# A fused attention and gated MLP kernel: a token moved to TensorE's queue, maxima turned by VectorE, a projection in 64-row tiles

## The chip, the cores and the metric

The kernel runs on one core of a Trainium2 chip. The core has five engines that work beside each other, each with its own instruction queue: TensorE (matmuls; PE in the profile, its weight loads PEld), VectorE (DVE), ScalarE (ACT), GpSimd (POOL) and SyncE (SP, which here only issues DMAs). They wait for each other through semaphores. Matmul results land in PSUM, which has eight banks of 128 x 512 numbers of 32 bits.

The metric is device time of one execution in microseconds. Three runs of the kernel before took 1590.16, 1590.88 and 1591.05; their median is 1590.88.

## The reference

Two branches read the same normalised rows. One is attention with 32 heads of 16 columns over 2048 rows, then a projection; the other is an MLP whose output gates the first.

```python
xn = _layernorm(x)                                  # x: 1 x 2048 x 512
q, k, v = split(xn @ wqkv)                          # 32 heads of 16
p = softmax(einsum("bhqd,bhkd->bhqk", q, k) * 16 ** -0.5)
s = einsum("bhqk,bhkd->bhqd", p, v) @ wo            # 512 x 512
g = silu(gelu(xn @ w1 + b1) @ w2 + b2)              # 512 x 1376 x 512
return x + s * g
```

## The kernel before, in words

Products of numbers of 32 bits are made from high and low parts: three matmuls (high by high, high by low, low by high) in the fast 32-bit form, summed in one PSUM bank. For scores the three products stand above each other in the contraction, 3 x 16 = 48 rows, so that one score matmul has 48 rows and uses one *row tile*, the upper or the lower 64 rows of TensorE's array (`a` = 0 or 1). [...]

The attention is cut into 32 *units* `u`: a group of four heads (`GH`), eight groups (`NG`), and a chunk of 512 query rows, four chunks (`NCH`). For a unit every score is made twice:

- **S**: queries on PSUM's partitions, keys along the columns, 128 x 512. VectorE takes the maximum of each half row (L185, `s_max`), and the maxima of a unit are reduced and negated (`nm`, L240) and split into high and low parts by POOL (`nmh`, L243 and L244).
- **T**: keys on the partitions, queries along the columns, with two more rows in the contraction (50 rows) that subtract the maximum of each query. ScalarE takes the exponential (L724, `t_one`). The result `PT` is multiplied with the values (**V**, L787, `pv_step`), four matmuls with 128 rows and 17 columns, side by side in columns; the seventeenth column gives the denominator.

For T the maxima must lie along a row, so the 128 x 32 tile `nmh` of a unit is turned. `s_end1` (L259) does this with a TensorE matmul against the identity into a PSUM bank, and `s_end2` copies the bank to SBUF (L265 by ScalarE during the first stage, L267 by VectorE later) and stores it to a scratch tensor `mh_d` (L268). `load_mh` later reads the two rows into the query tile `QT`. When `s_end1` runs is counted: a finished unit is put in `later` with a number of ticks.

There are three stages:

1. **First stage** (to about 480 us): layer norm, the matmuls for q, k, v and the MLP, in 64-row tiles, two row tiles interleaved by hand (`run`, `mm`, L573). `fill` puts S matmuls (`LEAD` = 144 steps' worth) between them when a count of matmuls is due; `ROWS` is the total of that count, and a turn in `fill` takes two places of it (`put`).
2. **Attention stage**: a loop over `n` of 512 steps. Each step works off a string of letters, `ORDER`: `TSXTTSTYV` while S remain to be made, `TTTTV` after. Four T make up one key block of a unit, V is the product for the step before. Of the three S tiles that a step makes, two are whole (S: both matmuls of a pair come at different places, one on each row tile) and the third is cut in halves: X writes one half of a bank from row tile 0, Y the other half from row tile 1. [...] This order is a *token*: an empty instruction on POOL (L217) that waits for X, and Y waits for it. POOL's small work on the maxima (`put_off`) is queued behind the token.
3. **Projection**: from step `DONE` = 492 the S are done. The first `NW` = 10 blocks of 128 rows are multiplied with `wo` inside the loop, each in two steps, with full 128-row matmuls (`w_mul`, L79), six a step after its four T. `load_gx` fetches the gate and the rows of x into a ring of four `gx` tiles, `w_token` rounds the attention output into high (ScalarE, L854) and low parts (POOL, L855), `gate` makes the silu factor (L847, L848), `w_out` multiplies from PSUM (VectorE, L883), adds x (POOL, L888) and stores. The other six blocks are done in the last steps and behind the loop.

Between V and the projection the denominators are handled: `o_move` moves them, `o_den` inverts them and sends each of four heads' rows back to 16 partitions with a DMA of its own (L819), `o_div` multiplies (L824).

The order on each engine is the order in which the program issues. PSUM banks are taken in turn: three for S (`s_tile`, `s_ring`), four for T (`t_tile`), one for V. A turn in the attention stage takes one of the T banks, one in the first stage one of the S banks.

Of the kernel before, what the change touches and what calls it, by code (L numbers as in the profile page):

```python
# [8 lines left out]
F32 = mybir.dt.float32  # L9
F32R = mybir.dt.float32r  # L10
AF = mybir.ActivationFunctionType
# [5 lines left out]
P = 128  # L17
S = 2048
D = 512
H = 32  # L20
DH = 16
KT = D // P
NT = S // P
CH = 512
NCH = S // CH
F = 1376
FT = (F + P - 1) // P
GH = 4
# [4 lines left out]
LEAD = 144  # L33
NW = 10
EARLY = 4
DONE = 492
FILL0 = 38
# [4 lines left out]
KB = 3  # L42
# [5 lines left out]
def fused(ctx: ExitStack, tc: tile.TileContext, x, wqk, wv, wo, w1, b1, w2, b2, out):  # L48
    nc = tc.nc
# [14 lines left out]
    den_d = dpool.tile([NG * NCH, GH, CH], F32, name="den_d")  # L64
    mh_d = dpool.tile([NG * NCH, 2, GH, CH], F32, name="mh_d")

    ident_r = keep.tile([P, P], F32R, name="ident_r")
# [13 lines left out]
            if then:  # L81
                then()

    QS, QT, MX, NM, MH = {}, {}, {}, {}, {}
    SYNC = mybir.DependencyInfo(mybir.DependencyClass.Sync, mybir.DependencyReason.DATA)
    qss = []
    NU = NG * NCH
# [3 lines left out]
    def s_tile(held=False):  # L91
        pool = s_ring.pop(0)
        if not held:
            s_ring.append(pool)
        return pool.tile([P, CH], F32, name="ps"), pool
# [57 lines left out]
    made = [0, 0]  # L153
    done = {u: 0 for u in range(NU)}
    later, ended, errands, sent = [], [], [], set()
# [5 lines left out]
    def flush():  # L161
        while later and later[0][0] <= 0:
            u = later.pop(0)[1]
            run_off()
            s_end1(u)
            s_end2(u)

    def at_of(job):
        u, st, p = job
# [24 lines left out]
    def s_whole(job, a):  # L194
        ps = s_tile()[0]
        s_mm(ps, job, a, 0, 0, CH)
        s_max(ps, job, a, slice(0, 2))
# [5 lines left out]
    jobs, whole, cut, put_off = [], [], [], []  # L203

    def s_op(op):
        if op == "S":
            if whole:
                s_whole(whole.pop(), 1)
            else:
                whole.append(jobs.pop(0))  # L210
                s_whole(whole[0], 0)
        elif op == "X":
            if not cut:
                cut[:] = [jobs.pop(0), 0]
            ps, pool = s_tile(True)
            x = s_mm(ps, cut[0], 0, 0, cut[1] * HC, HC)
            token = nc.gpsimd.nop().ins  # L217
            tc.add_manual_dep(token, x.name, SYNC, reason="row tile done")
            cut[2:] = [ps, pool, token]
            run_off()  # L220
        else:
            job, n, ps, pool, token = cut
            y = s_mm(ps, job, 1, HC, n * HC, HC)
            tc.add_manual_dep(y, token.name, SYNC, reason="other row tile")
            s_max(ps, job, slice(0, 2), n)
            s_ring.append(pool)
            cut[1] += 1
            if n:
                cut.clear()

    def run_off():
        while put_off:
            put_off.pop(0)()
# [21 lines left out]
    prog = {}  # L255

    def s_end1(u):
        pm = s_tile()[0] if "seen" in prog else t_tile()
        nc.tensor.matmul(pm[:2 * GH * NCH, :P], NM.pop(u).rearrange("p i a -> p (i a)"), ident_r, start=True, stop=True)  # L259
        MH[u] = pm  # L260

    def s_end2(u):
        mh = qring.tile([2 * GH * NCH, P], F32, name="mh", bufs=1)
        if "seen" in prog:
            nc.scalar.activation(mh, MH.pop(u)[:2 * GH * NCH, :P], AF.Copy)  # L265
        else:
            nc.vector.tensor_copy(mh, MH.pop(u)[:2 * GH * NCH, :P])  # L267
        nc.sync.dma_start(mh_d[u].rearrange("i j (q s) -> (i j q) s", s=P), mh)  # L268
        sent.add(u)

    sa = ExitStack()
# [19 lines left out]
    VQ = 3  # L291
    first = [[("v", t // NCH, t % NCH) for t in range(i, i + 4)] for i in range(NT - 4 * VQ, NT, 4)]
    qs = [(2, 0), (2, 2)] + [(g, 0) for g in range(3, NG)] + [(g, 2) for g in range(3, NG)]
    nu, pairs = len(ms) // 2, []
# [8 lines left out]
    for j in range(len(pairs)):  # L303
        for h in range(2):
# [4 lines left out]
            due = next((i for i in range(j, len(pairs)) if is_m[i]), len(pairs))  # L309
# [4 lines left out]
            n = 2 if nd < len(parts) and parts[nd][2] and ready - nd > room else 1  # L314
            n = max(n, need - 2 * (left - 1))
            while nd < ready and n > 0:
                c, f, k = parts[nd]
# [204 lines left out]
    qring = ctx.enter_context(tc.tile_pool(name="qring", bufs=2, side="right"))  # L522
# [16 lines left out]

    prog.update(n=0, pe=0, seen=0)  # L540
    writer = {}
    s_when, put, row = [], [0], [0, 0]
    ndown = sum(1 for e in plan if e[0] == "down")
    ROWS = 12 * (4 * VQ + 2 * len(pairs)) + 6 * ndown - 10 + 2 * LEAD - 2 * (LEAD // 16 - 1) - FILL0

    def fill(a):
        due = FILL0 + put[0] + sum(made) * ROWS // (4 * LEAD)
        if sum(made) < 4 * LEAD and row[a] >= due and (made[0] <= made[1]) == (a == 0):
            taken()
            if later and later[0][0] <= 0:  # L550
                put[0] += 2
                u = later.pop(0)[1]
                s_end1(u)
                s_end2(u)
                return
            s_one(a)
            row[a] += 1
            tick()

    def taken():  # L560
        prog["pe"] += 1
        s_when.append(prog["pe"])
        if len(s_when) > 2:
            prog["seen"] = max(prog["seen"], s_when[-3])
# [142 lines left out]
    def t_tile():  # L707
        turns[0] += 1
        if turns[0] < 5:
            pool = (ps_m, ps_x, ps_a, ps_b)[turns[0] - 1]  # L710
        else:
            pool = ps_m if turns[0] % 4 == 1 else ps_t
        return pool.tile([P, CH], F32, name="pst" if pool is ps_t else "ps")
# [46 lines left out]
    wb = ctx.enter_context(tc.tile_pool(name="work_b", bufs=2))  # L760
# [4 lines left out]
    wo_h = kp.tile([P, KT, D], F32R, name="wo_h")  # L765
    wo_l = kp.tile([P, KT, D], F32R, name="wo_l")

    WR = {}

    def load_wo(k):  # L770
        WR[k] = wb.tile([P, 2, D], F32, name="gx", bufs=4)[:, 0]
        nc.sync.dma_start(WR[k], wo[k * P:(k + 1) * P, :])

    def wo_high(k):
# [5 lines left out]
    PV, OS, DN, DR = {}, {}, {}, {}  # L780
# [18 lines left out]
    def o_rows(u, j):  # L799
        g, c = divmod(u, NCH)  # L800
        r0 = 64 * (g % 2) + DH * j
        return slice(r0, r0 + DH), c, g // 2
# [10 lines left out]
    def o_den(u):  # L813
        dr = DR.pop(u)
        nc.vector.reciprocal(dr, dr)
        nc.sync.dma_start(den_d[u].rearrange("j (a i) -> (j a) i", i=GH * CH // P), dr)
        DN[u] = wb.tile([P, CH], F32, name="dn", bufs=1)
        for j in range(GH):
            nc.sync.dma_start(DN[u][o_rows(u, j)[0]], den_d[u, j:j + 1].to_broadcast([DH, CH]))  # L819

    def o_div(u, eng):
        g, c = divmod(u, NCH)
# [3 lines left out]
    GX, OTS, PW, homes = {}, {}, {}, {}  # L826

    def home(i):
        if i not in homes:
            homes[i] = (slot(i, (P, KT, D)) if i < KB else  # L830
                        keep_r.tile([P, 2 * KT, D], F32, name="kt0"))
        return homes[i]

    def load_gx(t):
        i = 2 * (t % NCH)
        if t < NW:
            GX[t] = wb.tile([P, 2, D], F32, name="gx", bufs=4)
        elif t < NT - NCH:
            GX[t] = home(KB)[:, i:i + 2]
        else:  # L840
            GX[t] = home(1 + i // KT)[:, i % KT:i % KT + 2]
        nc.sync.dma_start(GX[t][:, 0], g_d[t * P:(t + 1) * P, :])
        nc.sync.dma_start(GX[t][:, 1], x[t * P:(t + 1) * P, :])
# [4 lines left out]
        nc.vector.scalar_tensor_tensor(g, e, 1.0, g, op0=OP.add, op1=OP.mult)  # L848

    def w_round(blocks, src, lo):  # L850
        oh = wb.tile([P, KT, P], F32R, name="oh", bufs=3)
        ol = wb.tile([P, KT, P], F32R, name="ol", bufs=3)
        n = len(blocks)
        nc.scalar.activation(oh[:, :n], src, AF.Copy)  # L854
        lo.tensor_sub(ol[:, :n], src, oh[:, :n].bitcast(F32))  # L855
        for i, b in enumerate(blocks):
            OTS[b] = (oh[:, i], ol[:, i])
# [12 lines left out]
    def w_mul(t, ks, parts=(0, 1)):  # L870
        if t not in PW:
            PW[t] = [ps_t.tile([P, CH], F32, name="pst") if NW <= t < NT - NCH or i else
                     ps_m.tile([P, CH], F32, name="ps") if t == NT - 1 else s_tile()[0]
                     for i, cs in enumerate(cols(t))]
        for i, cs in enumerate(cols(t)):
            if i in parts:
                for k in ks:
                    mm3(PW[t][i][:, :cs.stop - cs.start], OTS[t, k], (wo_h[:, k, cs], wo_l[:, k, cs]),
                        k == 0, k == KT - 1)

    def w_gate(t, i=0):
        gx, cs = GX[t], cols(t)[i]
# [14 lines left out]
    def at(n, f, *a, pos=3):  # L897
        todo.setdefault((n, pos), []).append((f, a))

    KS = tuple(range(KT))  # L900
# [21 lines left out]
            at(16 * u + (31 if u < NU - 2 else 22), o_div, u, nc.gpsimd)  # L922
    T3 = range(NT - NCH, NT)
    late = range(NW, NT)
    for t in range(NW):
        n = DONE + 2 * t
        at(n - 4, load_gx, t)
        at(n - 2, w_token, t)
        at(n, w_mul, t, KS[:2])
        at(n, gate, t)  # L930
        at(n + 1, w_mul, t, KS[2:])
        at(n + 1, w_out, t, nc.gpsimd)
    for i, t in enumerate(late):
        n = L - 2 * len(late) - 1 + 2 * i
        at(n - 4, load_gx, t)
# [8 lines left out]
    for n in range(L + 1):  # L944
        ua, ka = divmod(n, 16)
        want = due(n) - due(n - 1)
        i = 0
# [71 lines left out]
```

## Time and profile before

| what | us |
|---|---|
| median of three runs | 1590.88 |
| the profiled execution, whole | 1589.65 |
| its span, first to last instruction | 1587.9 |
| first exponential of the attention stage (L724) | 480.2 |
| last one | 1562.8 |
| turns of maxima (L259), 32, each on TensorE | 0.247 |
| POOL tokens (L217), 490, each | 0.017 |

The span lies 1.75 us inside the profiled execution's time. In a row of the timeline the columns are the start in us, the duration in us (of all merged instructions, if there are several), the engine (with q for its sequencer), the line, the operation, the tiles written and read, the shapes, a count, and in brackets the idle time of the engine before it and what ended that. A matmul's form `48*128 48x256` means 48 rows, 128 weight columns and 256 streamed columns. The end of a matmul is modelled, and matmuls overlap, so starts are safer than durations. In a row of the windows view, busy microseconds of each engine are followed by the count of instructions, and at the end stand the granted clock, the DMA share and GB/s. In a row for one source line, three durations (least, median, most, in ns) are followed by the first and last start.

### The profile page before, as it was taken

Reading aid. Unit: us, or ns where it says so; the run is one execution under the profiler, and the core shown is the slowest. Engines: PE = TensorE matmul, PEld = TensorE weight load, DVE = VectorE, ACT = ScalarE, POOL = GpSimd, SP = SyncE. Lnnn points to the kernel's source line nnn. Section 1 sums busy time; section 2 is a strip of 40 time slices with the busy share of each in tenths; the row PEclk is TensorE's granted clock in tenths of the full one; section 3 lists DMA queues with packets and bytes.
Section 4 is the critical chain, followed back from the end, with each engine's and each line's share of the span. In section 5 each row is a group of like instructions: output and inputs, shape, how many; then the busy total and the mean of one; then the engine's idle time right before and its main releaser. Section 6 shows DMA issues by size and latency. Waiting matters only on the chain.

```text
span 1587.9 us, 32482 instructions
## 1 busy us (share of the span) xinstructions
PE 1577.7 (99%) x12146; PEld 954.9 (60%) x12146; DVE 1382.6 (87%) x2267; ACT 1256.4 (79%) x2524; POOL 378.7 (24%) x398
## 2 busy tenths in 40 slices
PE   9999999999999999999999999999999999999998
PEld 7899989999995444444444444444444444444445
DVE  7489888888988999999999999999999999999734
ACT  4333433444339999999999999999999999999984
POOL 4145575755641001001100200100010000000144
PEclk9999999999999999999999999999999999999999
DMA  6625443354422113111511411221141111110262
GB/s 206 150 59 138 131 137 98 127 154 127 130 83 75 39 33 70 31 36 35 86 31 31 69 35 37 53 49 29 27 78 26 31 29 37 35 29 22 65 198 89
DMA packets 76798, 116.93 MB, mean 74 GB/s; under 512 B 25156, under 2 KB 26436, under 8 KB 75464
## 3 DMA queue, kind: packets, MB, share of 16 engines
q1 hardware_dynamic: 73180, 102.42, 23.4%
q0 software_dynamic: 3264, 12.35, 4.1%
q8 instruction: 96, 1.57, 0.4%
q14 instruction: 62, 0.51, 0.1%
q10 hardware_dynamic: 196, 0.07, 0.0%
HBM read 84.35 MB, written 25.97 MB: 69 GB/s over the span
## 4 chain that ended last, share of the span: by engine, by line
PE 98%; DVE 1%; DMA 0%; issue 0%; ACT 0%; SPq 0%; DVEq 0%; POOLq 0%; ACTq 0%
PE pv L787 32%; PE pst L722 22%; PE ps L573 13%; PE ps L179 9%; PE pst L573 7%; PE ps L722 7%; PE ps L79 4%; PE pv L573 2%; PE pst L79 1%; DVE slot L74 0%; DMA xt<-in_x 0%; DVE st L407 0%; PE pst L259 0%; PE ps L259 0%; DVE xn L421 0%
## 5 line engine op out<-in xcount | busy, mean ns | idle before, releaser
L185 DVE TENSOR_REDUCE mx<-ps 128x2 f32<-128x512 f32 x2048 | 1299.3, 685 | 137.3 <-PE ps L179 53.3
L724 ACT ACTIVATE slot<-pst 128x512 f32<-128x512 f32 x1533 | 833.3, 612 | 5.6 <-PE ps L179 1.1
L787 PE MATMUL pv<-slot,vsb 128*17 128x512 f32 (+1 forms) x4096 | 539.2, 598 | 0.0
L179 PE MATMUL ps<-kt,slot 48*128 48x512 f32 x1364 | 383.6, 370 | 0.1
L722 PE MATMUL pst<-qt,kt 50*128 50x512 f32 x1149 | 380.1, 431 | 0.5 <-DVE gt L655 0.3
L722 PEld LDWEIGHTS pst<-qt,kt 50*128 50x128 f32 x1149 | 191.5, 184 | 264.7 <-ACT slot L724 250.6
L724 ACT ACTIVATE slot<-ps 128x512 f32<-128x512 f32 x515 | 314.8, 612 | 10.3 <-PE pst L722 7.4
L179 PEld LDWEIGHTS ps<-kt,slot 48*128 48x128 f32 x1364 | 225.1, 184 | 2.1 <-POOLq L217 0.4
L573 PE MATMUL ps<-slot,w1h 64*128 64x512 f32 x1088 | 220.4, 393 | 0.0
L179 PE MATMUL ps<-kt,qz 48*128 48x512 f32 x512 | 214.7, 420 | 0.0
L179 PE MATMUL ps<-slot,slot 48*128 48x512 f32 x598 | 167.8, 368 | 0.0
L722 PE MATMUL ps<-qt,kt 50*128 50x512 f32 x387 | 164.1, 426 | 0.0
L573 PEld LDWEIGHTS ps<-slot,w1h 64*128 64x128 f32 x1088 | 153.0, 185 | 6.8 <-ACT junk L587 1.0
L573 PE MATMUL ps<-slot,w1l 64*128 64x512 f32 x544 | 143.0, 393 | 0.0
L367 POOL TENSOR_TENSOR hl<-hg,hh 128x512 fp32r<-128x512 f32 x76 | 96.9, 1298 | 131.5 <-ACT hh L366 92.6
L722 PE MATMUL pst<-qt,slot 50*128 50x512 f32 x384 | 120.1, 426 | 0.0
L787 PEld LDWEIGHTS pv<-slot,vsb 128*17 128x17 f32 (+1 forms) x4096 | 68.7, 96 | 82.8 <-issue 29.4
L587 ACT ACTIVATE junk<-ident_r 1x1 f32<-1x1 f32 x92 | 18.0, 196 | 126.1 <-PE pst L573 122.9
L722 PEld LDWEIGHTS ps<-qt,kt 50*128 50x128 f32 x387 | 71.1, 184 | 75.5 <-ACT slot L724 57.7
L722 PEld LDWEIGHTS pst<-qt,slot 50*128 50x128 f32 x384 | 65.9, 184 | 78.0 <-ACT slot L724 73.0
L179 PEld LDWEIGHTS ps<-kt,qz 48*128 48x128 f32 x512 | 93.7, 183 | 17.9 <-DVE mx L185 0.6
L179 PEld LDWEIGHTS ps<-slot,slot 48*128 48x128 f32 x598 | 98.7, 184 | 1.0
(150 smaller groups left out, 1659.4 us busy)
## 6 DMA issues: line engine op xcount, KB each, us to landing
raw<-in_w SPq DMA_DIRECT2D x88, 256.0 KB
qk_h<-hh SPq DMA_DIRECT2D x32, 256.0 KB
qk_l<-hl SPq DMA_DIRECT2D x32, 256.0 KB
qt<-qk_h SPq DMA_DIRECT2D x128, 64.0 KB
slot<-qk_h SPq DMA_DIRECT2D x92, 64.0 KB
xt<-in_x SPq DMA_DIRECT2D x16, 256.0 KB
g_d<-gt POOLq DMA_DIRECT2D x16, 256.0 KB, 3.0
qt<-qk_l SPq DMA_DIRECT2D x64, 64.0 KB
```

The costliest lines, as they stand in the source:

```text
L79: nc.tensor.matmul(ps, lhs[a], rhs[b], start=first and n == 0, stop=last and n == 2)
L179: return nc.tensor.matmul(ps[:, c0:c0 + w], QS[u][r, p, qi * P:(qi + 1) * P], kts[u // NCH % KB][p][r, k0:k0 + w], start=True, stop=True).ins
L185: nc.vector.tensor_reduce(MX[u][:, 2 * p:2 * p + 2, qi, ki][:, heads, parts], ps.rearrange("p (n c) -> p n c", c=HC), axis=AX.X, op=OP.max)
L367: nc.gpsimd.tensor_sub(hl, raw, hh.bitcast(F32))
L573: i = nc.tensor.matmul(ps, lhs[r], rhs[r], start=first, stop=last).ins
L587: i = nc.scalar.activation(junk[:, :1], ident_r[:1, :1].bitcast(F32), AF.Copy).ins
L722: nc.tensor.matmul(ps, kts[g % KB][p][r, k * P:(k + 1) * P], QT[u][r, p, :], start=True, stop=True)
L724: nc.scalar.activation(PT[u, k][:, 2 * p + a, :], ps, AF.Exp, scale=SCALE)
L787: nc.tensor.matmul(PV[u][32 * j:32 * j + w, :], vsb[:, k, h:h + w], PT[u, k][:, j, :], start=(k == 0), stop=(k == NT - 1))
```

## The change

Four things change.

- **The token.** X no longer issues an empty instruction on POOL. Y issues one on TensorE, directly ahead of its own matmul; it waits for X, and Y waits for it.
- **The turn.** `s_end1` turns the tile with one VectorE transpose of 128 x 32, which turns each block of 32 x 32 by itself, straight into SBUF; the store to `mh_d` follows that layout with pieces of 32 numbers. The matmul, the PSUM bank, the copy and `s_end2` go, and in `fill` the turn takes no places of the count any more.
- **The projection.** Blocks go in pairs over four steps. `w_half` issues the contraction in 64-row halves, row tile 0 for one block of the pair and row tile 1 for the other, four halves behind each of the step's first three T; after two steps the row tiles swap, behind a token on POOL (`turned`). The two blocks use two S banks.
- **Buffers and DMAs.** The ring of `gx` has three tiles and that of `oh` and `ol` four; every fourth block's `gx` goes elsewhere. The four broadcast DMAs of a unit's denominators become one.

```diff
@@ s_op
             x = s_mm(ps, cut[0], 0, 0, cut[1] * HC, HC)
-            token = nc.gpsimd.nop().ins
-            tc.add_manual_dep(token, x.name, SYNC, reason="row tile done")
-            cut[2:] = [ps, pool, token]
+            cut[2:] = [ps, pool, x]
             run_off()
         else:
-            job, n, ps, pool, token = cut
+            job, n, ps, pool, x = cut
+            token = nc.tensor.nop().ins
+            tc.add_manual_dep(token, x.name, SYNC, reason="row tile done")
             y = s_mm(ps, job, 1, HC, n * HC, HC)
             tc.add_manual_dep(y, token.name, SYNC, reason="other row tile")
@@ s_end1, s_end2
     def s_end1(u):
-        pm = s_tile()[0] if "seen" in prog else t_tile()
-        nc.tensor.matmul(pm[:2 * GH * NCH, :P], NM.pop(u).rearrange("p i a -> p (i a)"), ident_r, start=True, stop=True)
-        MH[u] = pm
...
+        mh = qring.tile([P, 2 * GH * NCH], F32, name="mh", bufs=1)
+        nc.vector.transpose(mh, NM.pop(u).rearrange("p i a -> p (i a)").bitcast(F32))
+        nc.sync.dma_start(mh_d[u].rearrange("i j (q b s) -> b (i j q) s", b=NCH, s=2 * GH * NCH), mh)
         sent.add(u)
@@ fill
-    ROWS = 12 * (4 * VQ + 2 * len(pairs)) + 6 * ndown - 10 + 2 * LEAD - 2 * (LEAD // 16 - 1) - FILL0
+    ROWS = 12 * (4 * VQ + 2 * len(pairs)) + 6 * ndown - 10 + 2 * LEAD - FILL0
@@ o_den
-        for j in range(GH):
-            nc.sync.dma_start(DN[u][o_rows(u, j)[0]], den_d[u, j:j + 1].to_broadcast([DH, CH]))
+        r0 = o_rows(u, 0)[0].start
+        nc.sync.dma_start(DN[u][r0:r0 + GH * DH], den_d[u].rearrange("j (o s) -> j o s", o=1).to_broadcast([GH, DH, CH]))
@@ load_gx
-        if t < NW:
-            GX[t] = wb.tile([P, 2, D], F32, name="gx", bufs=4)
+        if t < NW and i < 6:
+            GX[t] = wb.tile([P, 2, D], F32, name="gx", bufs=3)
         elif t < NT - NCH:
-            GX[t] = home(KB)[:, i:i + 2]
+            GX[t] = home(KB)[:, i - 6 * (t < NW):][:, :2]
@@ w_half, new
+    def w_half(t, part, third):
+        two = (t, t + 1)
+        if part == 0 and third == 0:
+            for b in two:
+                PW[b] = [s_tile()[0]]
+        side, ks = divmod(part, 2)
+        ops = [(k, i, j) for k in KS[2 * ks:2 * ks + 2] for i, j in ((0, 0), (0, 1), (1, 0))]
+        for n in (2 * third, 2 * third + 1):
+            for a in range(2):
+                b, r, (k, i, j) = two[a ^ side], slice(64 * a, 64 * a + 64), ops[n]
+                op = nc.tensor.matmul(PW[b][0], OTS[b, k][i][r], (wo_h, wo_l)[j][r, k], start=part == 0 and n == 0,
+                                      stop=part == 3 and n == 5).ins
+                if part == 2 and n == 0:
+                    tc.add_manual_dep(op, turned[t].name, SYNC, reason="other row tile")
+        if part == 1 and third == 2:
+            turned[t] = nc.gpsimd.nop().ins
+            tc.add_manual_dep(turned[t], op.name, SYNC, reason="row tile done")
@@ the plan of the loop
-    for t in range(NW):
+    for t in range(0, NW, 2):
         n = DONE + 2 * t
-        at(n - 4, load_gx, t)
-        at(n - 2, w_token, t)
-        at(n, w_mul, t, KS[:2])
-        at(n, gate, t)
-        at(n + 1, w_mul, t, KS[2:])
-        at(n + 1, w_out, t, nc.gpsimd)
+        for b in range(2):
+            at(n - 3 + b, load_gx, t + b)
+            at(n - 2 + b, w_token, t + b, pos=3 * (1 - b))
+            at(n + b, gate, t + b)
+        for part in range(4):
+            for third in range(3):
+                at(n + part, w_half, t, part, third, pos=third)
+        for b in range(2):
+            at(n + 3, w_out, t + b, nc.gpsimd)
```

More of the change, by code (lines that the diff above doesn't have):

```diff
@@ L82, in mm3 @@
                 then()
-    QS, QT, MX, NM, MH = {}, {}, {}, {}, {}
+    QS, QT, MX, NM = {}, {}, {}, {}
     SYNC = mybir.DependencyInfo(mybir.DependencyClass.Sync, mybir.DependencyReason.DATA)
@@ L165, in flush @@
             s_end1(u)
-            s_end2(u)
     def at_of(job):
@@ L257, in s_end1 @@
     def s_end1(u):
-        pm = s_tile()[0] if "seen" in prog else t_tile()
-        nc.tensor.matmul(pm[:2 * GH * NCH, :P], NM.pop(u).rearrange("p i a -> p (i a)"), ident_r, start=True, stop=True)
-        MH[u] = pm
[L262 to L268, printed above, removed]
+        mh = qring.tile([P, 2 * GH * NCH], F32, name="mh", bufs=1)
+        nc.vector.transpose(mh, NM.pop(u).rearrange("p i a -> p (i a)").bitcast(F32))
+        nc.sync.dma_start(mh_d[u].rearrange("i j (q b s) -> b (i j q) s", b=NCH, s=2 * GH * NCH), mh)
         sent.add(u)
@@ L541, in fused @@
     writer = {}
-    s_when, put, row = [], [0], [0, 0]
+    s_when, row = [], [0, 0]
     ndown = sum(1 for e in plan if e[0] == "down")
-    ROWS = 12 * (4 * VQ + 2 * len(pairs)) + 6 * ndown - 10 + 2 * LEAD - 2 * (LEAD // 16 - 1) - FILL0
+    ROWS = 12 * (4 * VQ + 2 * len(pairs)) + 6 * ndown - 10 + 2 * LEAD - FILL0
     def fill(a):
-        due = FILL0 + put[0] + sum(made) * ROWS // (4 * LEAD)
+        due = FILL0 + sum(made) * ROWS // (4 * LEAD)
         if sum(made) < 4 * LEAD and row[a] >= due and (made[0] <= made[1]) == (a == 0):
@@ L550, in fill @@
             if later and later[0][0] <= 0:
[L551 to L555, printed above, removed]
+                s_end1(later.pop(0)[1])
             s_one(a)
@@ L770, in load_wo @@
     def load_wo(k):
-        WR[k] = wb.tile([P, 2, D], F32, name="gx", bufs=4)[:, 0]
+        WR[k] = wb.tile([P, 2, D], F32, name="gx", bufs=3)[:, 0]
         nc.sync.dma_start(WR[k], wo[k * P:(k + 1) * P, :])
@@ L850, in w_round @@
     def w_round(blocks, src, lo):
-        oh = wb.tile([P, KT, P], F32R, name="oh", bufs=3)
-        ol = wb.tile([P, KT, P], F32R, name="ol", bufs=3)
+        oh = wb.tile([P, KT, P], F32R, name="oh", bufs=4)
+        ol = wb.tile([P, KT, P], F32R, name="ol", bufs=4)
         n = len(blocks)
@@ L879, in w_mul @@
                         k == 0, k == KT - 1)
+    turned = {}
+    def w_half(t, part, third):
[15 more added lines that the diff above has]
+            tc.add_manual_dep(turned[t], op.name, SYNC, reason="row tile done")
     def w_gate(t, i=0):
```

## The prediction

> **What bounds the kernel now.** I read the totals and the chain of waits first, then three stretches in the windows view (one each of the first stage, the attention stage and the projection steps), then single steps in the timeline.
>
> ```profile
> PE 1577.7 (99%) x12146; PEld 954.9 (60%) x12146; DVE 1382.6 (87%) x2267; ACT 1256.4 (79%) x2524; POOL 378.7 (24%) x398
> PE 98%; DVE 1%; DMA 0%; issue 0%; ACT 0%; SPq 0%; DVEq 0%; POOLq 0%; ACTq 0%
> 200.00:300.00 100.00, 100.00 (x832) 90.41 (x829) 89.23 (x142) 39.27 (x89) 62.98 (x57) 1.00 0.37 119
> 1000.00:1100.00 100.00, 100.00 (x782) 47.75 (x782) 92.47 (x154) 99.59 (x198) 7.76 (x13) 1.00 0.25 46
> 1520.00:1540.00 20.00, 20.00 (x112) 9.39 (x111) 8.64 (x10) 17.61 (x35) 9.95 (x7) 1.00 0.63 206
> ```
>
> TensorE carries the chain in all three. In the first stage it starts 832 matmuls in 100 us, 0.120 us each, two row tiles at once. In the attention stage ScalarE looks as full, but its busy time is a union of overlapping records. One step of that stage:
>
> ```profile
> 902.34 1.66 ACT L724 ACTIVATE slot<-pst 128x512 f32<-128x512 f32 x3
> 902.38 0.50 PE L179 MATMUL ps<-kt,slot 48*128 48x512 f32 x1
> 902.72 0.28 PE L179 MATMUL ps<-kt,slot 48*128 48x256 f32 x1
> 903.00 0.18 PEld L722 LDWEIGHTS pst<-qt,kt 50*128 50x128 f32 x1
> 903.10 0.18 PEld L179 LDWEIGHTS ps<-kt,slot 48*128 48x128 f32 x1
> 903.21 0.27 PE L179 MATMUL ps<-kt,slot 48*128 48x256 f32 x1
> 903.43 1.05 PE L787 MATMUL pv<-slot,vsb 128*17 128x512 f32 x8
> 904.41 0.50 PE L722 MATMUL pst<-qt,kt 50*128 50x512 f32 x1
> 904.36 1.68 ACT L724 ACTIVATE slot<-pst 128x512 f32<-128x512 f32 x3
> ```
>
> The step is 904.36 − 902.34 = 2.02 us. Score matmuls run from 902.38 to 903.43, pv from 903.43 to 904.41, and the next score matmul starts at once, so TensorE has no pause. The first half tile (X, 902.72) ends at 903.00. The second half (Y) has its weights at 903.10, and pv starts 0.33 after them. Y is the last matmul before pv, so what delays Y by more than a small slack delays the step.
>
> **The Y token.** [...] The token between them is an empty instruction:
>
> ```profile
> L217 POOLq EVENT_SEMAPHORE  x490: 17/17/17, 485.0 to 1497.2; - x164
> L179 PEldq EVENT_SEMAPHORE  x59: 51/51/51, 525.1 to 1453.4; - x59
> 526.16 0.28 PE L179 MATMUL ps<-slot,slot 48*128 48x256 f32 x1
> 526.45 0.18 PEld L722 LDWEIGHTS ps<-qt,kt 50*128 50x128 f32 x1
> 526.62 0.18 PEld L179 LDWEIGHTS ps<-slot,slot 48*128 48x128 f32 x1
> 526.93 0.13 PEld L787 LDWEIGHTS pv<-slot,vsb 128*17 128x17 f32 x8
> ```
>
> Now it is POOL's, 17 ns; afterwards it is TensorE's own, where this kind takes 51 ns. Between X's end (903.00) and Y's weights (903.10) lie two semaphore hops and 17 ns, so a hop is (0.10 − 0.017) / 2 = 0.042. With the token on TensorE there are still two hops (X's completion to TensorE's sequencer, the token's semaphore to Y), and 51 ns: 0.135, so Y's weights come 0.035 later. TensorE's sequencer has not run ahead at that place. The second group of rows is a step with two such instructions between T3 and Y, both without a real wait: from T3's weights (526.45) to Y's is 0.17, where the step above has 903.10 − 903.00 = 0.10, and pv comes 526.93 − 526.16 = 0.77 after X instead of 0.71. Y later by 0.08 cost the step 0.06, so up to 0.02 of a delay is free.
>
> The bounds for one token are thus nothing (were it read before X ends and its semaphore needed no second hop, Y's weights would stand where they are) and the 0.06 that two of them cost. I take 0.030 per step: the 0.035 of the sum of hops, with little of the slack taken off, because I assume that the semaphore leaves after the 51 ns and not within them. 490 × 0.030 = **+14.7 us** (0 to +29.4). Queued behind the waiting token in TensorE's sequencer are Y, the four pv matmuls and the next step's first T; all wait with it, and ScalarE and VectorE wait for those. A gain is bounded by T3, which ends beside Y now; I set it to nothing. POOL's queue loses 490 tokens; one of them stood behind a subtraction and held Y:
>
> ```profile
> 1497.31 0.18 PEld L179 LDWEIGHTS ps<-kt,slot 48*128 48x128 f32 x1 [0.39 <-POOLq L217]
> ```
>
> That goes. But the pairing moves one more ScalarE rounding (0.65 us by the L854 row below) into the neighbouring step, where ScalarE is full. Together **−0.3 us** (−0.4 to +0.3).
>
> **The turn of the maxima.** Each of 32 units loses a TensorE matmul against the identity, a copy out of PSUM and a PSUM bank.
>
> ```profile
> 161.79 0.39 PE L573 MATMUL pv<-w2l,hh 64*128 64x512 f32 x1
> 162.12 0.25 PE L259 MATMUL ps<-ident_r,nmh 128*32 128x128 f32 x1
> 162.29 0.49 PE L573 MATMUL pst<-w2h,hl 64*128 64x512 f32 x1
> 162.30 0.50 PE L573 MATMUL pv<-w2h,hl 64*128 64x512 f32 x1
> 162.63 0.40 PE L573 MATMUL pst<-w2h,hh 64*128 64x512 f32 x2
> L259 PE MATMUL pst<-ident_r,nmh x18: 246/247/248, 529.9 to 1502.2; 128*32 128x128 f32 x18
> L267 DVE COPY mh<-pst x18: 269/269/279, 530.3 to 1502.5; 32x128 f32<-32x128 f32 x18
> 528.95 1.05 PE L787 MATMUL pv<-slot,vsb 128*17 128x512 f32 x8
> 531.24 0.62 PE L787 MATMUL pv<-slot,vsb 128*17 128x512 f32 x4
> L240 DVE TENSOR_REDUCE nm<-mx x32: 273/275/286, 108.0 to 1498.7; 128x16 f32<-128x128 f32 x32
> ```
>
> First stage: from the 64-row matmul at 161.79 to that at 162.63 there are three starts (162.29, 162.30, 162.63). At 0.120 each they would take 0.36 and took 0.84; I put down 0.45 as lost to leaving the 64-row tiles and coming back. 8 units × 0.45 = **−3.6 us**. Attention stage: such a step lasts 531.24 − 528.95 = 2.29 instead of 2.02, so 0.27; the matmul alone is 0.247, and where a step also waits for something else less is won. 24 × 0.22 = **−5.3 us** (−6.5 to −4). VectorE's turn of 128×32 is not in the trace; the nearest rows are 0.27 to 0.28, below it nothing. It replaces a copy of 0.27 on VectorE in the attention stage and lies beside a TensorE-bound stage before, so it costs nothing; were that cover gone, 32 × 0.28 = 9 us. It now waits for POOL in VectorE's queue, with the score maxima behind it. The store of the maxima goes out in 128-byte pieces; it is read back for a later unit.
>
> **The projection in 64-row tiles**, 20 steps.
>
> ```profile
> 1534.95 0.50 PE L722 MATMUL ps<-qt,kt 50*128 50x512 f32 x1
> 1534.95 0.73 PE L722 MATMUL pst<-qt,kt 50*128 50x512 f32 x3
> 1535.61 0.50 PE L79 MATMUL ps<-wo_h,oh 128*128 128x512 f32 x1
> 1535.95 0.39 PE L79 MATMUL ps<-wo_l,oh 128*128 128x512 f32 x1
> 1536.88 0.40 PE L79 MATMUL ps<-wo_h,ol 128*128 128x512 f32 x1
> 1537.21 1.05 PE L787 MATMUL pv<-slot,vsb 128*17 128x512 f32 x8
> 1538.19 0.49 PE L722 MATMUL ps<-qt,kt 50*128 50x512 f32 x1
> 1534.68 0.65 ACT L854 ACTIVATE oh<-slot 128x512 fp32r<-128x512 f32 x1
> 1537.31 0.69 DVE L883 SCALAR_TENSOR_TENSOR gx<-ps,gx 128x512 f32<-128x512 f32 x1 [1.72 <-PE ps L79]
> ```
>
> A step is 1538.19 − 1534.95 = 3.24, of which 2.26 is before pv: 0.66 for four T, 1.60 for six full matmuls, one change of tiling between. The four T are two on each row tile, issued as row 1, 1, 0, 0, and all start within 0.73 − 0.39 = 0.34: the row tiles run beside each other without keeping that order. Afterwards each row tile streams two T and six halves: 8 × 0.240 (two of the first stage's 0.120) = 1.92, plus what the score part of the step at 902 has over its 3.5 such pairs, 1.05 − 0.84 = 0.21: 2.13. So −0.13 × 20 = **−2.6 us**, taken as −2.5 (−4 to +5). The token at the swap of the row tiles is POOL's, but a pv of 0.98 lies before the matmul that waits for it. The two banks of a pair are emptied by VectorE (L883, 0.69 each) under the next pv.
>
> [...]
>
> **Other edits.** The four broadcast DMAs of a denominator become one and the gx ring loses a buffer (two tiles go elsewhere): SP's and the DMAs' time, behind TensorE's; nothing.
>
> **Sum**, from the profiled execution's 1589.65: +14.7 − 0.3 − 3.6 − 5.3 − 2.5 = +3.0, 1592.65. The median of the runs is 1.23 above that execution: **1593.9 us** beside 1590.88.
>
> **Rivals.**
> - *The token is free* (faster). Its instruction is read while X still streams, and T3 sets pv's start. For it: T3's weights at 903.00 have 0.43 to pv, Y's 0.33, both near the end. Against it: Y follows its token by the same small gap in the step shown. Without the 14.7: 1590.88 − 11.7 = 1579.2; with a tenth or two of it, up to 1582.
> - *The token costs as two did* (slower). Place: TensorE's sequencer between T3 and Y; price 0.06 a step, +29.4, so 1590.88 + 29.4 − 11.7 = 1608.6. It is slower than before from 11.7 / 490 = 0.024 a step on. For it: 0.06 was measured; against: that was for two.
> [...]
> - *The turn stalls VectorE*: it has 7.5 us spare in 100 of the attention stage (92.47 busy), so a wait for POOL under 0.1 per step is hidden; beyond that banks come late. Up to the 9 us above, 1603.
>
> **How the numbers follow.** Forecast 0.42, free token 0.33, dear token 0.17, program order 0.04, VectorE 0.04. The forecast's own range is 1589 to 1599 (0.020 to 0.040 a step). The 8-in-10 range reaches to most of both sides: 1578.5 to 1605. About 0.2% (3.2 us) is what a measurement of this kernel can tell from no change. Faster: the free token and the lower tail of the forecast (0.04), 0.37. Same: 0.23, all from the forecast. Slower: the rest of it and the other three, 0.40.
>
> **What would show it.** In the step view: Y's weights at 0.10 after X's end or at 0.135, and the attention step at 2.02 or 2.05. Row L259 and the steps of 2.29 gone; the first stage shorter by 3 to 4 us at the first exponential. A projection step of 3.1 instead of 3.24, its four T spread over it. Wrong if Y's weights don't move, if VectorE shows idle time before the turn, or if the projection step is at or over 3.24.

## The result and the profile after

The changed kernel took 1603.67 us (median of four runs, 1603.26 to 1604.36) against 1590.79: a ratio of 1.0082, 95% interval 1.0065 to 1.0099. It is slower, as forecast, and inside the range of 1578.5 to 1605. It lies outside the likeliest case's own range of 1589 to 1599: the forecast was +3 us and the chip says +12.9.

The totals and the chain of waits of the changed kernel:

```profile
PE 1585.4 (99%) x12234; PEld 975.9 (61%) x12234; DVE 1376.5 (86%) x2275; ACT 1268.4 (79%) x2516; POOL 378.0 (24%) x398
PE 97%; DVE 1%; ACT 1%; issue 1%; DMA 0%; POOL 0%; SPq 0%; DVEq 0%; ACTq 0%
```

TensorE still carries the chain, but 1% of it is now "issue", time in which TensorE waited for nothing that the profile shows. Before it was 0%. The same three windows as before:

```profile
200.00:300.00 100.00, 100.00 (x842) 91.30 (x840) 90.55 (x145) 39.05 (x87) 64.21 (x59) 1.00 0.38 122
1000.00:1100.00 100.00, 95.58 (x720) 46.02 (x719) 86.00 (x142) 93.40 (x183) 7.72 (x13) 0.98 0.27 46
1520.00:1540.00 20.00, 20.00 (x162) 10.57 (x164) 4.69 (x9) 18.15 (x35) 8.20 (x7) 1.00 0.42 136
```

The first stage makes 842 matmuls in 100 us where it made 832. The attention window has 720 where it had 782, TensorE was idle for 4.4 us in it, and the granted clock was 0.98. So the gain is in the first stage and the loss in the attention stage, and part of that loss is not spread over the steps. A plain step of the changed kernel in the timeline:

```profile
1037.33 0.49 PE L709 MATMUL ps<-qt,kt 50*128 50x512 f32 x1
1037.67 0.28 PE L178 MATMUL ps<-slot,slot 48*128 48x256 f32 x1
1037.93 0.18 PEld L709 LDWEIGHTS pst<-qt,kt 50*128 50x128 f32 x1
1038.09 0.18 PEld L178 LDWEIGHTS ps<-slot,slot 48*128 48x128 f32 x1
1038.40 1.05 PE L774 MATMUL pv<-slot,vsb 128*17 128x512 f32 x8
1039.39 0.50 PE L709 MATMUL ps<-qt,kt 50*128 50x512 f32 x1
```

X starts at 1037.67 and ends at 1037.95. Y's weights come at 1038.09, 0.14 after it (0.10 before the change), the product 0.73 after X's start (0.71 before), and the step takes 2.06. That is the predicted hop. The very next step is another matter:

```profile
1040.08 0.39 PE L709 MATMUL pst<-qt,kt 50*128 50x512 f32 x1
1044.89 0.18 PEld L178 LDWEIGHTS ps<-slot,slot 48*128 48x128 f32 x1 [4.73 <-issue]
1045.27 1.91 PE L774 MATMUL pv<-slot,vsb 128*17 128x512 f32 x8
1047.11 0.29 PEld L709 LDWEIGHTS ps<-qt,kt 50*128 50x128 f32 x1 [1.68 <-issue]
1048.73 1.05 PE L774 MATMUL pv<-slot,vsb 128*17 128x512 f32 x8
```

From one product to the next (1038.40 to 1045.27) 6.87 us pass, and 3.46 to the one after. TensorE stops ahead of Y for 4.4 us with no engine to blame, and when it goes on, a weight load takes 0.29 instead of 0.18 (the granted clock is 0.53 over the 3.6 us behind the stop, as the last section shows). The DMA view of two neighbouring stretches names what is missing (the queue, its packets, megabytes and share):

```profile
DMA packets 1087, 2.47 MB, mean 105 GB/s; under 512 B 463, under 2 KB 463, under 8 KB 895
q0 software_dynamic: 288, 1.57, 54.2%
q1 hardware_dynamic: 799, 0.89, 29.1%
```

```profile
q1 hardware_dynamic: 325, 0.07, 22.1%
q8 instruction: 1, 0.02, 3.7%
```

The first fence is the stretch from 1018.5 to 1041.9, in which no packet of the instruction queue q8 starts. The second is 1041.9 to 1044.5: the packet starts at 1041.96 and ends at 1043.51, and TensorE goes on at 1044.89. The profile calls q8 an instruction queue. It has 98 packets of 16 KB in the changed kernel, and TensorE has 25,222 weight loads, matmuls and instructions of its sequencer, 257 to a packet; I take the packets for blocks of TensorE's program. So one can ask of each packet how far TensorE had got when it started. I count the rows of TensorE begun before packet j and subtract 256 j. In the kernel before, what is left stays between 160 and 239 over all 96 packets, so 256 to a packet fits. Steps are taken from one product to the next: "plain" ones are those under 2.075 us, "long" ones those over 2.43, and the last column is what the long ones have over 2.06. Steps and packets are counted from step 8 to step 489:

```
kernel         plain step   rows past 256 j     past 410   long steps, us over
               mean, us     median   largest    of all
before         2.030        192      234        0 of 61     0    0
changed        2.063        354      449        12 of 63    11   14.0
```

Before, a packet starts when TensorE is some 190 rows past, whatever the step; in the changed kernel it starts up to 257 rows (449 − 192), a whole block, later than that. Each of the eleven long steps stands at a packet that was past 410 (two of them at the same); the other two such packets stand at steps of 2.35 and 2.26. I read the stops as TensorE having nothing left to run. In the first stage both kernels have nearly the same median (201 and 204), and in the projection steps, where no token stands in TensorE's queue, it is back to about 200.

The turns by the row of their source line, and the product (V) by the rows of its line in the changed kernel and in the kernel before:

```profile
L258 DVE STREAM_TRANSPOSE mh<-nmh x32: 200/203/208, 116.9 to 1520.4; 128x32 f32<-128x32 f32 x32
L774 PE MATMUL pv<-slot,vsb x4096: 589/603/1061, 478.1 to 1577.7; 128*17 128x512 f32 x183, 128*32 128x512 f32 x13
```

```profile
L787 PE MATMUL pv<-slot,vsb x4096: 592/593/618, 483.1 to 1564.4; 128*17 128x512 f32 x183, 128*32 128x512 f32 x13
```

A turn takes VectorE 0.203 us. The first product starts at 478.1, 5.0 earlier, the last ones 13.3 later. The longest of these matmuls rose from 618 to 1061 ns: the eight over 618 all start between 1045.27 and 1046.12, under the lowered clock (0.53) behind the longest standstill. A projection step in the timeline:

```profile
1537.76 0.50 PE L709 MATMUL ps<-qt,kt 50*128 50x512 f32 x1
1538.33 0.40 PE L880 MATMUL ps<-wo_h,ol 64*128 64x512 f32 x1
1538.56 0.40 PE L709 MATMUL pst<-qt,kt 50*128 50x512 f32 x1
1538.80 0.39 PE L709 MATMUL pst<-qt,kt 50*128 50x512 f32 x1
1539.03 0.39 PE L880 MATMUL ps<-wo_l,oh 64*128 64x512 f32 x1
1539.49 0.40 PE L709 MATMUL pst<-qt,kt 50*128 50x512 f32 x1
1539.82 0.62 PE L774 MATMUL pv<-slot,vsb 128*17 128x512 f32 x4
```

The four T are spread over the step, the slots of the row tiles follow each other by 0.23, and 2.06 lie between the first T (1537.76) and the product (1539.82).

### The profile page after: what moved, and what is told of

It reads as the page before. It is cut to its first block, busy times and chain, and to the rows that moved or that the text cites. A ratio compares the mean times of both kernels' runs of the same rounds, so it can differ in the third digit from the quotient of the medians.

```text
span 1601.2 us, 32455 instructions
## 1 busy us (share of the span) xinstructions
PE 1585.4 (99%) x12234; PEld 975.9 (61%) x12234; DVE 1376.5 (86%) x2275; ACT 1268.4 (79%) x2516; POOL 378.0 (24%) x398
## 4 chain that ended last, share of the span: by engine, by line
PE 97%; DVE 1%; ACT 1%; issue 1%; DMA 0%; POOL 0%; SPq 0%; DVEq 0%; ACTq 0%
PE pv L774 32%; PE pst L709 16%; PE ps L709 14%; PE ps L560 12%; PE ps L178 11%; PE pst L560 7%; PE pv L560 2%; PE ps L79 1%; PE ps L880 1%; PE pst L79 1%; DVE slot L74 0%; ACT slot L711 0%; DMA xt<-in_x 0%; DVE st L398 0%; POOL ol L842 0%
## 5 line engine op out<-in xcount | busy, mean ns | idle before, releaser
L711 ACT ACTIVATE slot<-pst 128x512 f32<-128x512 f32 x1533 | 810.3, 616 | 2.0 <-PE ps L709 0.8
L774 PE MATMUL pv<-slot,vsb 128*17 128x512 f32 (+1 forms) x4096 | 545.7, 599 | 1.2 <-issue 1.2
L178 PE MATMUL ps<-kt,slot 48*128 48x512 f32 x1364 | 396.6, 379 | 0.0
L709 PE MATMUL pst<-qt,kt 50*128 50x512 f32 x1149 | 303.8, 399 | 0.5 <-DVE gt L642 0.3
L709 PEld LDWEIGHTS pst<-qt,kt 50*128 50x128 f32 x1149 | 211.2, 185 | 29.9 <-ACT slot L711 11.0
L709 PE MATMUL ps<-qt,kt 50*128 50x512 f32 x387 | 191.1, 496 | 0.1
L178 PE MATMUL ps<-slot,slot 48*128 48x512 f32 x598 | 174.4, 379 | 4.4 <-issue 4.4
L242 POOL CAST nmh<-nm 128x16 fp32r<-128x16 f32 x32 | 6.4, 198 | 500.9 <-DVE nm L239 500.9
L709 PE MATMUL pst<-qt,slot 50*128 50x512 f32 x384 | 98.9, 398 | 0.0
```

What stands on the lines that cost most here:

```text
L178: return nc.tensor.matmul(ps[:, c0:c0 + w], QS[u][r, p, qi * P:(qi + 1) * P], kts[u // NCH % KB][p][r, k0:k0 + w], start=True, stop=True).ins
L242: nc.gpsimd.tensor_copy(hl[:, 0], nm)
L709: nc.tensor.matmul(ps, kts[g % KB][p][r, k * P:(k + 1) * P], QT[u][r, p, :], start=True, stop=True)
L711: nc.scalar.activation(PT[u, k][:, 2 * p + a, :], ps, AF.Exp, scale=SCALE)
L774: nc.tensor.matmul(PV[u][32 * j:32 * j + w, :], vsb[:, k, h:h + w], PT[u, k][:, j, :], start=(k == 0), stop=(k == NT - 1))
```

## The experiments

Theory A was formed from these rows: the token costs once by its hops and once more because TensorE's sequencer, held at it in each step, gets its blocks of instructions late. Theory B blamed the DMAs that the change alters (the store of the maxima in 128-byte pieces, the single broadcast DMA of a denominator) for the late packets.

**POOL's token in the changed kernel.**

```diff
 x = s_mm(ps, cut[0], 0, 0, cut[1] * HC, HC)
-cut[2:] = [ps, pool, x]
+token = nc.gpsimd.nop().ins
+tc.add_manual_dep(token, x.name, SYNC, reason="row tile done")
+cut[2:] = [ps, pool, token]
...
-job, n, ps, pool, x = cut
-token = nc.tensor.nop().ins
-tc.add_manual_dep(token, x.name, SYNC, reason="row tile done")
+job, n, ps, pool, token = cut
```

> The changed kernel with the token given back to POOL; all else of the change stays. Theory A: the token in TensorE's queue costs twice. Once by its hops, about 0.0325 us in each plain attention step (382 plain steps, 12.4 us), and once more because TensorE's sequencer no longer gets ahead of TensorE, so blocks of 256 instructions are asked for late and TensorE stands still in eleven steps (14 us together). Both go: 1603.7 - 12.4 - 14 = 1577 us; no attention step longer than 2.5 us, and the instruction queue's packets start when TensorE is 180 to 240 instructions past 256 times their number, as in the kernel before. Theory B: the eleven standstills come from the DMAs that the change alters (maxima stored in 128-byte pieces, one broadcast DMA for a denominator), which hold up the instruction packets: only the hops go, 1603.7 - 12.4 = 1591 us, and the late packets stay.

1577.19 us, ratio 0.9915 (0.9901 to 0.9928): theory A, and the fastest kernel of the study. Plain steps of 2.030, packets at a median of 189 and never past 225, no long step. A step in its timeline:

```profile
900.31 1.05 PE L774 MATMUL pv<-slot,vsb 128*17 128x512 f32 x8
901.63 0.28 PE L178 MATMUL ps<-kt,slot 48*128 48x256 f32 x1
902.01 0.18 PEld L178 LDWEIGHTS ps<-kt,slot 48*128 48x128 f32 x1
902.34 1.05 PE L774 MATMUL pv<-slot,vsb 128*17 128x512 f32 x8
```

Y's weights stand 0.10 after X's end (901.91) again and the step at 2.03. The altered DMAs are all still there, so theory B falls. POOL's token has one cost of its own, at step 489. The pairing puts a second subtraction ahead of the token in POOL's queue, and that one waits for ScalarE's second rounding, which ends at 1488.32:

```profile
1488.43 0.18 PEld L178 LDWEIGHTS ps<-kt,slot 48*128 48x128 f32 x1 [1.39 <-POOLq L216]
```

That step takes 3.48, where the kernel before takes 2.49 and the changed kernel 2.07. The changed kernel pays most of it one step later (4.00 for 3.04), where TensorE waits for a low part from POOL.

**The token alone**: the reverse edit, made on the kernel before.

> The kernel before with the token moved to TensorE's queue and nothing else of the change. Theory A: hops 12.4 us and standstills of about 14 us: 1590.8 + 26.4 = 1617 us (1612 to 1620), with instruction packets up to 450 instructions past 256 times their number. Theory B: hops alone, 1603 us, instruction packets as before.

1621.12 us, ratio 1.0192 (1.0178 to 1.0206), 1.1 us over theory A's range. The largest count of rows past is 449 again. From the first product to that of step 489 it needs 1041.0 where the kernel before needs 1012.1; 16.6 of the 28.9 are ten long steps, 12.3 the rest. Its longest stop, in the view of TensorE's waits (line waited for, total us, times, longest):

```profile
PE pv L787 <- issue: 7.0, 3, 4.9
```

**The turn alone**: `s_end1` with VectorE's transpose, the store and the count `ROWS` of the change, on the kernel before.

> The kernel before with the maxima turned by VectorE and nothing else of the change. From the changed kernel's trace: attention begins 5.0 us earlier and the 24 later turns are worth about 5 us. Theory A: 1590.8 - 10 = 1581 us. Theory B (the store in 128-byte pieces takes part in the standstills): some of the 14 us come back, 1585 to 1595 us, with steps over 2.5 us.

1579.79 us, ratio 0.9932 (0.9918 to 0.9945). The first product starts at 477.7, and from there to step 489 it takes 1007.3, 4.7 less than before. No step is long: the store in small pieces costs nothing that can be seen.

**The token on TensorE for every second tile, on POOL for the others.**

```diff
-cut[2:] = [ps, pool, x]
+if own[0]:
+    token = x
+else:
+    token = nc.gpsimd.nop().ins
+    tc.add_manual_dep(token, x.name, SYNC, reason="row tile done")
+cut[2:] = [ps, pool, token]
...
+if own[0]:
+    x, token = token, nc.tensor.nop().ins
+    tc.add_manual_dep(token, x.name, SYNC, reason="row tile done")
+own[0] ^= 1
```

> The changed kernel with the token in TensorE's queue for every second third tile and on POOL for the others. Theory A in the form that the sequencer catches up in any step without its own token: hops halve (6.2 us), no block is asked for more than about 66 instructions (two steps) later than in the kernel before, no standstill: 1577 + 6 = 1583 us. Theory A in the form that each token adds its share of lateness: both halve, 1577 + 13 = 1590 us, with late packets past 400.

1581.4 us. Half of the hops stay (plain step 2.043), and the lateness is gone altogether: median 199, largest 260. One step without a token in TensorE's queue between two with one was enough here for the packets to start about as early as in the kernel before (192, 234).

**Is it the instruction or its wait?** Four kernels put one more empty instruction into TensorE's queue ahead of Y, on the kernel before and beside POOL's token. The next POOL token waits for it, so that it has a reader.

```diff
 job, n, ps, pool, token = cut
+bare.append(nc.tensor.nop().ins)
...
+if bare:
+    tc.add_manual_dep(token, bare.pop().name, SYNC, reason="bare")
```

The first waits for nothing. The second has `tc.add_manual_dep(bare[0], x.name, ...)` for the X of the same step, the third and fourth the same for the Y of one and of two steps before.

> The kernel before, POOL's token kept, with one more empty instruction in TensorE's queue ahead of each Y that waits for nothing (490 more instructions of 51 ns). Theory A1: it is the wait at the token that holds TensorE's sequencer back. Then blocks of instructions are asked for as in the kernel before (TensorE at most 240 instructions past 256 times their number), there is no standstill, and only the 51 ns count, if they lie on the path at all: 1591 to 1606 us (0 to 0.03 us a step). Theory A2: any instruction that the sequencer handles by itself makes it fall behind: late blocks past 400, standstills of some 14 us, 1605 to 1620 us.

> The same extra instruction, now waiting for X as the change's token does; Y still waits for POOL's token alone. Theory A1 and A2: late blocks past 400, standstills of 10 to 18 us, and 0.02 to 0.035 us more in a plain step: 1608 to 1622 us. Rival A3: what costs is that Y waits for a semaphore of its own sequencer, not that the sequencer waits for X: blocks in time, plain step within 0.01 us of before, 1591 to 1596 us.

> The kernel before with POOL's token and the extra instruction in TensorE's queue, which now waits for the Y of the step before (ended about 1.9 us earlier in TensorE's time). Theory A4: the wait matters by how far it lets the sequencer get ahead; here by one step (33 instructions) where X of the same step allowed about half a step and no wait at all gave a median block request 226 past: median between 226 and 300, hardly any past 410, 1596 to 1602 us. Theory A5: any wait of the sequencer for TensorE's own completion makes blocks late, satisfied or not: median 350, standstills, 1608 to 1622 us.

> The same with the Y of two steps before (66 instructions of freedom). Theory A4: as without any wait, median 226 (up to 240), no standstill, 1595 to 1599 us. Theory A5: as with the wait for X, median 350, 1608 to 1622 us.

They took 1596.51, 1617.84, 1596.41 and 1596.51 us. The row of the first, and two of TensorE's waits in the second:

```profile
L225 PEldq EVENT_SEMAPHORE  x489: 51/51/51, 485.9 to 1501.6; - x163
```

```profile
PE pv L791 <- issue: 4.9, 5, 2.8
PE ps L179 <- issue: 3.7, 2, 2.0
```

All four have a plain step of 2.046 or 2.047, so 51 ns more in the sequencer cost 0.017 a step, and the wait adds nothing to that (A1 had expected 0.02 to 0.035). But the wait for the X of the same step makes the packets late (median 350, 13 past 410, 22.5 us in long steps), while with no wait, or a wait for what ended a step or two earlier, the median is 226 to 229 and nothing is long. Theories A2, A3 and A5 fall. A4 stands in so far as the wait matters by how lately its event was due; a graded lateness with one step of freedom was not seen.

**X one place earlier**, `TXSTTSTYV` for `TSXTTSTYV`: with the change's token, with POOL's token, and with POOL's token in every second step.

> The changed kernel with X one place earlier (ahead of S on its row tile instead of behind it), token in TensorE's queue as in the change. If the token costs because X has only just ended when the sequencer reads it, X now ends about 0.24 us (a whole tile) earlier, the token is passed without a wait, the plain step falls from 2.063 to 2.03 us, the sequencer gets ahead of TensorE again and blocks are late by less than 400: 1577 to 1585 us. If the cost is that of the instruction itself, wherever X ends, nothing changes: 1604 us. A third way: X's and Y's bank is held 0.24 us longer and VectorE empties the banks later, which would show as VectorE idle time and as a plain step over 2.063.

> The changed kernel with POOL's token and X one place earlier. Y is then no longer held by its token at all; T3, whose weights wait for ScalarE, still sets when the product starts. If T3 alone sets it: no change against POOL's token with X in its old place, 1577 us. If Y had been the later of the two: up to 0.02 us a step less, 1567 to 1577 us. If the bank is short: more than 1577.

> The changed kernel with POOL's token, and X one place earlier in every second step only. With X earlier in all steps they went 2.00 and 2.13 us by turns: the short one shows what Y's place costs, the long one waits for the bank that VectorE empties last. If the bank's lateness is paid by the step behind and VectorE catches up in a step of the old order: steps of 2.00 and 2.03 by turns, 490 x 0.015 = 7 us less than 1577.2, 1570 us. If the debt is paid in full by the step behind: 2.00 and 2.06 or more, 1577 us. If it depends on which of the two steps has X earlier: 2.13 against 2.00, 1590 us as before.

They took 1604.28, 1590.01 and 1586.51 us. With POOL's token the steps now go 2.00 and 2.13 by turns, and the timeline of a long one shows why:

```profile
900.29 0.50 PE L709 MATMUL ps<-qt,kt 50*128 50x512 f32 x1
900.89 0.18 PEld L178 LDWEIGHTS ps<-kt,slot 48*128 48x128 f32 x1 [0.18 <-DVE mx L184]
901.23 0.28 PE L178 MATMUL ps<-kt,slot 48*128 48x256 f32 x1
901.44 1.05 PE L774 MATMUL pv<-slot,vsb 128*17 128x512 f32 x8
```

The second S waits 0.18 for a bank that VectorE has not emptied, since the first S, and so VectorE's work, now comes later. The debt is more than what was won: the kernel that moves X in every second step alone mostly goes 2.00 and 2.12 all the same, and none of the three ways expected of it came. POOL's token with X in its old place stays the best. The first of the three says something else: its short steps take 2.010, against 2.008 with POOL's token, so with X earlier the hop is almost free (0.002), and yet the packets are as late as before (median 357, 16.0 us in long steps). Its time is the 1604 of the way in which nothing changes, but by luck: most of the hop went and the wait for the bank came in its place. Hop and lateness are two costs, and the second isn't cured by 0.24 us.

**The projection alone** (with the broadcast DMA and the buffers, POOL's token, TensorE's turn).

> The kernel before with the projection in 64-row tiles, the single broadcast DMA of a denominator and the changed buffers, without the turn of the maxima and with POOL's token. By the difference of POOL's-token kernel (1577.2) and the turn alone (1579.8): 1590.6 - 2.6 = 1588 us, all of it in the projection steps (3.24 to 3.05 us each, first of them 0.4 longer). If the parts lean on each other: 1590.6 or more.

1587.3 us, ratio 0.9982 (0.9973 to 0.9992). The parts add up: −2.8 for this and −10.9 for the turn (1579.79 against 1590.65) make −13.7, and the kernel with both is 13.5 under the kernel before. The −2.8 holds the longer wait at step 489 (3.50 for 2.49); what the broadcast DMA and the buffers do by themselves was not run.

## Why the prediction came out as it did

The terms in microseconds. The stretches run between products: the first product, that of step 489, that of step 490 and the last.

| term | predicted | measured | from |
|---|---|---|---|
| turn, first stage | −3.6 | −5.0 | first product 483.1 to 478.1 |
| turn, attention | −5.3 | −4.7 | turn alone, first product to step 489 (23 of the 24 turns): 1007.3 for 1012.1 |
| token's hops | +14.7 | +12.9 | changed less POOL's token, same stretch: 1034.36 − 1007.45, less the long steps |
| standstills | none | +14.0 | long steps over 2.06 |
| blocked Y at step 489 | −0.3 | −0.4 | step 2.49 to 2.07 |
| projection | −2.5 | −3.6 | step 490 to the last: 66.3 to 62.8; 0.3 of it is the 24th turn (turn alone: 66.0) |
| sum | +3.0 | +13.2 | span: 1587.9 to 1601.2, +13.3 |

**The token's hops: right.** 0.030 a step was taken and the plain step rose from 2.030 to 2.063; the steps that wait for something else anyway pay less. That a signal leaves after the 51 ns and needs a second hop was an assumption. The runs split it: 0.017 are the instruction itself (no wait, no signal that Y needs), the remaining 0.016 come with Y waiting for it. All kernels here keep Y behind X; no run shows what the two do without that order.

**What failed** is the sentence on what is queued behind the token: "Queued behind the waiting token in TensorE's sequencer are Y, the four pv matmuls and the next step's first T; all wait with it". It listed the instructions that wait and left out the packets of the queue q8. Where the sequencer stopped in each step for an event of that same step, they started up to 257 rows late, and at the latest of them TensorE stood still, for 4.4 us at 449 rows. That it had run out of instructions is my reading of these counts. The 14.0 us were in no term, and they are more than the whole miss of 10.2: the other terms come to −0.8 where +3.0 was forecast. So it is luck that the change came out slower, as forecast. Its token's hops alone would have left it where the kernel before is, and the slowdown came from a cost that the prediction didn't have. Late blocks with a wait for X in TensorE's queue in every step, and none without it, are shown: four kernels have that wait and are late, and no other is. Why a packet starts late, whether the sequencer asks for it late or something holds the request, the trace does not show, and no run settles it.

**The turn: right, its first-stage part mis-sized.** "I put down 0.45 as lost to leaving the 64-row tiles and coming back"; it measured 5.0 / 8 = 0.63 a unit. VectorE's 0.203 lies within the bounds, and no idle time stands before the turn: the rival in which it stalls VectorE did not happen.

**The projection: right in kind.** 2.06 before the product where 2.13 was worked out, and steps of 3.04 to 3.06. The eight slots of a row tile were run beside each other, 0.23 apart. One thing was not in the sum: in the first of these steps TensorE waits for POOL's low part:

```profile
1517.12 0.50 PE L880 MATMUL ps<-wo_h,ol 64*128 64x512 f32 x1 [0.44 <-POOL ol L842]
```

That step takes 4.00 instead of 3.60.

**The rivals.** The free token fell. "The token costs as two did", 0.06 a step, comes near in price (26.9 over 490 steps are 0.055), but for another cause: its steps would all be 2.09, and they are 2.063 with eleven stops. The gain of 11.7 that it was set against was really 13.5. No run shows the program order that 0.04 of the chances went to; the projection steps took 3.04 to 3.06, less than the 3.24 before.

## What to carry to other kernels

An empty instruction that waits was not free in the queue of the engine that sets the pace, even where its hop was nearly hidden: 490 of them cost 13 us by their hops and 14 us by blocks of instructions that came late. The same token on POOL, which is 24% busy, saves both, and the rest of this change is then worth 0.85%. Where a profile has idle time put down to "issue", look at when the instruction queue's packets start against how far the engine has got.

## What was not expected of the hardware

- TensorE stood still for 4.4 us at a packet that started at 449 rows, 257 past the median of 192 before, and 449 is the largest count in all four kernels that wait for X in every step. From these counts I estimate that TensorE had about one block in store beyond the point where a packet starts in the kernel before.
- After the stop of 4.4 us the granted clock was lowered, to 0.53 in the mean of 3.6 us. The windows view of the changed kernel around it:

```profile
1040.50:1044.90 4.40, 0.01 (x1) 0.01 (x1) 0.74 (x2) 1.49 (x4) 0.00 (x0) 1.00 0.51 69
1044.90:1048.50 3.60, 3.60 (x16) 1.60 (x17) 1.22 (x2) 0.56 (x2) 0.08 (x1) 0.53 0.10 36
1048.50:1060.00 11.50, 11.50 (x92) 5.25 (x89) 10.47 (x18) 11.25 (x24) 1.20 (x1) 1.00 0.01 3
```

The clock is 0.53 in the 3.6 us that follow the stop and full again behind them, so the stop costs more than its length; shorter stops of 0.3 and 0.8 us in this kernel left the clock at 1.00. In other runs the clock was 0.50 for 3.4 us after a stop of 2.0 us in the kernel whose added instruction waits for X, shown here, and halved after one of 1.3 us (1189.23 to 1190.56) in the changed kernel with X earlier, but not after one of 1.7 us (911.41 to 913.08) in the token alone. So in these runs the length of a stop alone does not decide it.

```profile
573.28:575.28 2.00, 0.00 (x1) 0.03 (x2) 0.60 (x2) 1.26 (x3) 0.42 (x2) 1.00 0.35 97
576.62:580.03 3.41, 3.41 (x20) 1.48 (x16) 2.44 (x4) 2.06 (x4) 0.00 (x0) 0.50 0.00 0
```

- The median lateness of the packets has no middle: a wait for X each step 350 rows, the same wait in every second step 199, a wait for a Y that ended a step earlier 229, no wait 226. Single packets do: in the changed kernel they range from 215 to 449.
